# Score rows for the softmax maximum: from the rounded operands alone, in half-array pairs with one reduction for both heads

## The chip, the cores and the metric

The kernel runs on one core of a Trainium2 chip. The metric is the device time of one execution in microseconds. Three runs of the kernel before took 1128.65, 1129.16 and 1133.55 us; the median is 1129.16 us. One further execution was recorded by the profiler: it took 1131.61 us, of which the span from its first to its last instruction is 1129.9 us. Every duration below comes from that one execution.

## The reference

An attention with normalised queries and keys feeds a mixture of experts with one expert per token. Inputs are float32, as is the output.

```
q, k, v: (8, 12, 448, 64)            # batch, heads, sequence, head size
q_n = q / sqrt(mean(q*q) + 1e-6) * g_q ; k_n likewise with g_k
scores = q_n @ k_n.T / 8
scores = scores - max(scores)         # along the keys
attn = exp(scores) ; attn /= sum(attn) + 1e-9
x = (attn @ v), heads side by side    # 3584 tokens of 768
logits = x @ w_gate + modality_bias[modality_id]
e = argmax(logits) ; gate = softmax(logits)[e]
out[token] = gate * (relu(x[token] @ w1[e]) @ w2[e])   # 8 experts, 768 -> 1024 -> 768
```

The maximum that is subtracted cancels when the row is divided by its sum, up to the 1e-9; it only has to be near the true one so that the exponentials stay in range.

## The kernel before

**Attention** runs in 48 units (`NU`), each a pair of heads of one batch element. A unit is worked on over seven steps of a plan, one step for each block `j` of the transposed scores: `st(u, j)` makes 128 rows of keys by 448 queries in PSUM, with the rounded and the remaining parts of the operands and minus the row maximum as an extra row of the contraction (hence matmuls of 65 rows), and ScalarE takes the exponential. Block 3 holds the last 64 keys of each head together. `av(u, c)` multiplies the exponentials with the values in the array's column halves, `sums` and `gates` use its column quarters, `tr` and `xt` transpose, `mt` transposes the maxima.

**The maximum** has to be known before `st` of the same unit, and is made one unit ahead or more by `sa(u, j)` (L810): a second product of queries and keys, not transposed, 128 queries by 448 keys into one PSUM bank, and a VectorE reduction along the keys into column `j` of `mx`. There are seven of them in a unit: three for either head, and one (`j == 3`) that takes the last 64 queries of both heads with a block-diagonal left operand `qm`. For the others the contraction has 128 rows: rows 0 to 63 of `qq` are the rounded queries of head 0, rows 64 to 127 a copy of them that a DMA moved there, and `kk` holds the rounded keys in one half and their remainders in the other. Only unit 0 (`u < PLAN["early"]`) contracts over the 64 rows of the rounded operands alone, because the moved halves would be late there. The left and right operands are `fp32r`, the accumulated scores float32.

**PSUM.** `ps_a` is a pool of two one-bank buffers. Every `sa` takes the next one, and so do `xtr` (the transposes of token rows in the second half, L464), `route_mm` for the last batch element, and the small paths `half_slot` and `small_slot`.

**The order** is written by hand: inside `manual_schedule`, each engine executes in the order in which the Python emits. `put(when("sa", u) + j, "sa", u, jj)` (L1139 to L1142) gives each `sa` its step: unit `u`'s block `j` at step 7u - 14 + j. In a step TensorE gets `st` first, then `sa`, then `av`, `sums`, `gates`, `tr`, `mt`, `xt`; VectorE gets the subtractions and other evacuations that are due, and the reduction of `sa` last. `PLAN` holds the numbers.

**The expert part** follows in 14 slots (`NSTAT`) of 256 tokens, written by hand too, and a tail whose length depends on the data. In a slot `mm1_half` (L485, tile `ph`) makes the hidden layer, `mm2_step` (L515, tile `py`) the output in 16 steps. After steps 9, 11 and 13 `xtr` transposes two of the next slot's six token blocks on TensorE (tile `px`, 128 by 512 in one bank), ScalarE writes the rounded part `xh`, and VectorE the remainder `xl` (tile `xw` in the profile). ScalarE and VectorE split the next slot's weights (`w1w`) in between, in their own program order.

Of the kernel before, what the change touches and what calls it, by code (L numbers as in the profile page):

```python
# [9 lines left out]
F32 = mybir.dt.float32  # L10
# [22 lines left out]
ET = mybir.EngineType  # L33
PLAN = {'rtj': 6, 'rushat': 36, 'av': (1, 1, 4, 6), 'xt': 4, 'xte': (2, 5), 'sm': 2, 'la': 6, 'rc': 9, 'csv': (1,), 'csj': (3, 6), 'csd': (1, 1), 'cse': (2, 1), 'sa': 14, 'mt': 6, 'tk': 21, 'tq': 18, 'nq': 26, 'nk': 26, 'sk': 49, 'sq': 50, 'rs': 48, 'ld': 58, 'first': {('sq', 0): -22, ('sk', 0): -22, ('nk', 0): -21, ('nq', 0): -20, ('sq', 1): -21, ('sk', 1): -21, ('sq', 2): -20, ('sk', 2): -20, ('nk', 1): -18, ('nq', 1): -18, ('tk', 0): -18, ('tq', 0): -18, ('sa', 0): -14, ('tk', 1): -13, ('tq', 1): -11, ('sa', 1): -7, ('mt', 0): -6, ('tk', 2): -8, ('tq', 2): -8, ('nq', 2): -14, ('nk', 2): -14, ('nq', 3): -2, ('nk', 3): -1, ('sq', 3): -8, ('sk', 3): -8, ('sq', 4): -9, ('sk', 4): -9, ('sq', 6): -6, ('sk', 6): -4, ('sk', 7): -7, ('sq', 8): 5, ('sk', 8): 5, ('nk', 7): 15, ('nq', 9): 31, ('tq', 3): 4, ('mt', 1): 0, ('nq', 5): 10, ('mt', 8): 50, ('rs', 0): -21, ('rs', 2): -18, ('nq', 8): 35, ('rs', 5): -7, ('mt', 2): 8, ('nq', 7): 18, ('mt', 5): 30, ('sk', 9): 15, ('tk', 9): 43, ('mt', 6): 36, ('nq', 6): 13, ('sa', 5): 22, ('rs', 7): 0, ('rs', 8): 6, ('mt', 4): 22, ('nk', 4): 4, ('ld', 9): 6, ('tk', 5): 15}, 'rs0': {0: 0, 2: 1, 5: 0, 7: 0, 8: 2}, 'sastep': 1, 'start': -22, 'warm': {5: 2, -6: 16, -12: 4, -7: 2, -9: 4, -21: 4}, 'warmn': 2, 'early': 1, 'late0': 1, 'pmp0': 2, 'ramp': 10, 'pmp': (0, 0, 1, 1, 1, 0, 1), 'nv': [(2, 1)], 'pmpa': (1, 0, 1, 0, 1, 1, 1), 'rush': (1, 1, 1), 'ps': [(7, 1)], 'pa': [(6, 0), (6, 1), (5, 1), (5, 0)], 'rtr': 6, 'sml': 4}
MANUAL = {ET.PE, ET.DVE, ET.Activation, ET.Pool, ET.SP}
# [31 lines left out]
def kernel(  # L67
# [396 lines left out]
    def xtr(s, xr, g):  # L464
        ps = ps_a.tile([128, 2, TB], F32, tag="a", name=f"px{s}_{g}")
        for i in range(2):
            for t in range(2):
                PE.transpose(ps[:, i, 128 * t : 128 * t + 128], xr[t][:, 2 * g + i], idn)  # L468
# [79 lines left out]
    def half_slot(s):  # L548
# [3 lines left out]
        def turn(jj):  # L552
            pt = ps_a.tile([128, 2, TB], F32, tag="a", name=f"pt{s}_{jj}")
# [23 lines left out]
    def small_slot(s, xr):  # L577
# [68 lines left out]
    if True:  # L646
# [162 lines left out]

        def sa(u, j):  # L810
            t = T[u]
            if j == 0:
                t["mx"] = mx_b[u % 2]
            ps = ps_a.tile([128, 512], F32, tag="a", name=f"sa{u}_{j}")
            if j == 3:
                PE.matmul(ps[:, :S], lhsT=qm_b[u % 2], rhs=hi_b[u % 2][1], start=True, stop=True)
            else:
                h = j // 4
                a = 128 * j - h * S
                r = slice(0, 128) if u >= PLAN["early"] else (LO, HI)[h]  # L820
                PE.matmul(ps[:, :S], lhsT=t["qq"][r, h, a : a + 128], rhs=t["kk"][h][r], start=True, stop=True)  # L821
# [301 lines left out]
        def put(n, *what):  # L1123
            plan.setdefault(n, []).append(what)
# [203 lines left out]
        for s in range(NSTAT):  # L1328
# [34 lines left out]
            for b_ in range(16):  # L1363
# [80 lines left out]
```

## Time and profile before

| what | value |
|---|---|
| median of three runs | 1129.16 us |
| the profiled execution, and its span | 1131.61 us, 1129.9 us |
| granted TensorE clock, mean over the span | 0.982 |
| TensorE matmul busy | 1076.3 us, 95% of the span, 6678 instructions |
| TensorE weight load busy | 837.3 us, 74% |
| VectorE busy | 859.6 us, 76%, 1598 instructions |
| ScalarE busy | 824.8 us, 73% |
| GpSimd busy | 662.7 us, 59% |

Attention fills the span up to about 580 us, the expert slots the rest up to about 1098 us, and the tail the last 30 us. A busy share is the union of the recorded durations of an engine. The duration of a matmul includes the time in which its data travel through the array, so that matmuls which follow each other without a gap overlap in the records by more than 0.1 us; what a matmul costs is read from the start of one to the start of the next. The timeline view merges equal neighbours into one row with a count.

### The profile page before, as it was taken

To read this page: it belongs to the slowest core of one execution; us is meant where nothing else is said; L and a number is where in the kernel's file an instruction comes from. 1 tells how busy PE (TensorE), PEld (TensorE's weight loads), DVE (VectorE), ACT (ScalarE), POOL (GpSimd) and SP (SyncE) were. 2 spreads that over 40 slices of the span, in tenths; PEclk is the share of its full clock that TensorE was granted. 3 is DMA by queue.
4 is the path that set the end of the run, shared out by engine and by line. 5 is a ranking of instruction groups with operands and counts; after the bars stand their busy time and mean duration, and the time that the engine had idled before them with its cause. 6 is when DMAs were issued, how large, how long until landed. Compare 5 with 4: busy or idle time off the path is not lost. (4 is left out here: it accounts for less than half of the span.)

```text
span 1129.9 us, 20043 instructions
## 1 busy us (share of the span) xinstructions
PE 1076.3 (95%) x6678; PEld 837.3 (74%) x6678; DVE 859.6 (76%) x1598; ACT 824.8 (73%) x1605; POOL 662.7 (59%) x665
## 2 busy tenths in 40 slices
PE   7799999999999999999999989999999999999993
PEld 6655555555555555555569889999999999999981
DVE  4577788888889877889689978767776677776770
ACT  6778888788778788776677577667876677766870
POOL 4477777778777778787865464354234433445430
PEclk8899999999999999999999999999999999999997
DMA  6656676677667777665823202111160111111360
GB/s 167 156 131 162 144 180 162 167 172 168 154 167 156 168 157 171 152 144 111 238 106 109 43 29 71 29 57 57 43 265 29 58 42 57 32 40 57 109 194 11
DMA packets 127970, 131.79 MB, mean 117 GB/s; under 512 B 68891, under 2 KB 122607, under 8 KB 126320
## 3 DMA queue, kind: packets, MB, share of 16 engines
q1 hardware_dynamic: 110212, 88.58, 33.5%
q0 software_dynamic: 17616, 41.80, 11.7%
q8 instruction: 57, 0.93, 0.4%
q14 instruction: 57, 0.47, 0.1%
q10 hardware_dynamic: 28, 0.01, 0.0%
HBM read 148.74 MB, written 22.38 MB: 151 GB/s over the span
## 5 line engine op out<-in xcount | busy, mean ns | idle before, releaser
L485 PE MATMUL ph<-xw,w1w 128*128 128x256 f32 x2016 | 247.6, 284 | 3.0 <-DVE hlw L52 2.3
L485 PEld LDWEIGHTS ph<-xw,w1w 128*128 128x128 f32 x2016 | 245.4, 193 | 5.0 <-DVE hlw L52 2.5
L52 DVE TENSOR_REDUCE at_hlw<-sa 128x1 f32<-128x448 f32 x336 | 206.7, 617 | 44.5 <-PE sa L821 23.3
L52 DVE TENSOR_TENSOR w1w<-r,w1w 128x256 fp32r<-128x256 f32 x360 | 220.3, 670 | 14.5 <-ACT w1w L52 14.4
L52 ACT CAST w1w<-r 128x256 fp32r<-128x256 f32 x360 | 224.7, 724 | 2.7 <-DMA r<-in_moe_w_dram,ta_wi 2.7
L849 PE MATMUL st<-w1w 128*128 128x448 f32 (+1 forms) x480 | 177.1, 418 | 3.8 <-ACT r2w L52 3.5
L52 ACT ACTIVATE hhw<-ph 128x512 fp32r<-128x512 f32 x56 | 33.5, 597 | 124.8 <-PE ph L485 110.5
L849 PEld LDWEIGHTS st<-w1w 128*128 128x128 f32 (+1 forms) x480 | 85.6, 192 | 48.2 <-ACT r2w L52 21.5
L821 PE MATMUL sa<-w1w 128*128 128x448 f32 (+1 forms) x288 | 110.3, 384 | 9.6 <-DVE at_hlw L52 5.0
L52 ACT ACTIVATE r2w<-st 128x448 f32<-128x448 f32 x168 | 90.1, 542 | 37.6 <-PE st L849 32.1
L52 POOL TENSOR_TENSOR r2w<-r2w 128x448 f32<-128x448 f32 (+1 forms) x72 | 83.4, 1158 | 55.4 <-DVE r2w L52 17.9
L515 PE MATMUL py<-w2lw,hhw 128*128 128x384 f32 x448 | 113.9, 335 | 0.0
L849 PE MATMUL st<-w1w,w2ha 65*128 65x448 f32 x288 | 101.9, 374 | 2.8 <-DMA w1w<-xw 2.5
L52 POOL DMA_INDIRECT out_dram<-yw,lb_oi x22 | 26.8, 1220 | 123.0 <-ACT yw L52 120.0
L52 POOL TENSOR_TENSOR xrw<-r,at_hlw 112x512 f32<-112x512 f32 x95 | 97.4, 1045 | 2.2 <-PE tr L750 1.8
L52 ACT ACTIVATE at_w2lw<-st 128x448 f32<-128x448 f32 x168 | 89.3, 541 | 9.0 <-PE st L849 4.0
L515 PEld LDWEIGHTS py<-w2lw,hhw 128*128 128x128 f32 x448 | 80.9, 188 | 0.0
L52 DVE SCALAR_TENSOR_TENSOR hlw<-ph,hhw 128x512 fp32r<-128x512 f32 x56 | 38.6, 690 | 53.8 <-ACT hhw L52 47.7
L52 ACT ACTIVATE w1w<-tr,gs 64x448 fp32r<-64x448 f32 x96 | 60.4, 629 | 24.8 <-DVE xw L52 24.2
L52 POOL TENSOR_TENSOR r2w<-r2w,at_w2lw 64x448 f32<-64x448 f32 (+1 forms) x48 | 55.4, 1153 | 31.9 <-DVE r2w L52 15.6
L52 ACT ACTIVATE xrw<-r 112x512 f32<-112x512 f32 (+1 forms) x124 | 64.7, 527 | 10.1 <-DMA r<-in_k_dram 7.8
L821 PEld LDWEIGHTS sa<-w1w 128*128 128x128 f32 (+1 forms) x288 | 55.4, 192 | 22.5 <-DVE at_hlw L52 10.2
(297 smaller groups left out, 2300.7 us busy)
## 6 DMA issues: line engine op xcount, KB each, us to landing
w1w<-xw SPq DMA_DIRECT2D x312, 112.0 KB
r<-in_q_dram SPq DMA_DIRECT2D x48, 224.0 KB
r<-in_k_dram SPq DMA_DIRECT2D x48, 224.0 KB
w2ha<-xw SPq DMA_DIRECT2D x72, 112.0 KB
x_d<-at_w2hb SPq DMA_DIRECT2D x8, 672.0 KB
x_d<-yw SPq DMA_DIRECT2D x8, 672.0 KB
r2w<-in_v_dram SPq DMA_DIRECT2D x48, 96.0 KB
at_w2lw<-in_v_dram SPq DMA_DIRECT2D x48, 96.0 KB
```

The costliest lines, as they stand in the source:

```text
L52: return fn(*a, **kw)
L485: PE.matmul(ps[:, i], lhsT=lt_, rhs=rt_[:, c], start=n == 0, stop=n == 17)
L515: PE.matmul(ps[n][:, :384], lhsT=lt_[:, j, 128 * t : 128 * t + 128], rhs=rt_[:, 384 * n : 384 * n + 384], start=j == 0 and m == 0, stop=j ...
L821: PE.matmul(ps[:, :S], lhsT=t["qq"][r, h, a : a + 128], rhs=t["kk"][h][r], start=True, stop=True)
L849: PE.matmul(ps[:, :S], lhsT=l, rhs=t["qq"][:, h] if first else t["ql"][:, h], start=first and (j != 3 or h == 0), stop=not first and (j != ...
```

## The change

Four things change.

1. **`sa` works on both heads at once.** It is called four times a unit instead of seven. For `i` = 0, 1, 2 it issues two matmuls of 64 contraction rows each: head 0 with rows 0 to 63 of `qq` and `kk[0]`, head 1 with rows 64 to 127 of `qq` and `kk[1]`, which are the rounded operands; the remainders of the keys no longer enter the maximum. The two write to the two banks of one tile. Call 3 is the block-diagonal matmul as before.
2. **One reduction for both maxima.** VectorE reduces the two banks in one instruction, 128x2 out of 128x2x448.
3. **The steps.** `sastep` goes, and `'sas': (0, 2, 5, 3)` comes: calls 0, 1, 2 stand in steps 0, 2 and 5 of the seven, the block-diagonal call in step 3. Unit 0 has them in four steps in a row.
4. **One PSUM tile.** The pool `ps_a` has a single buffer `pa` of two banks. `bank_a()` hands out one bank and the other in turn, to call 3 of `sa` and to all other users of the pool.

```diff
-    ps_a = ctx.enter_context(tc.tile_pool(name="ps_a", bufs=2, space=PSUM))
+    ps_a = ctx.enter_context(tc.tile_pool(name="ps_a", bufs=1, space=PSUM))
...
+    pa = ps_a.tile([128, 2, 512], F32, tag="a", name="pa")
+    turn_a = [0]
+    def bank_a():
+        turn_a[0] ^= 1
+        return pa[:, turn_a[0]]
...
     def xtr(s, xr, g):
-        ps = ps_a.tile([128, 2, TB], F32, tag="a", name=f"px{s}_{g}")
+        ps = bank_a().rearrange("p (i t) -> p i t", i=2)
...
-        def sa(u, j):
+        def sa(u, i):
             t = T[u]
-            if j == 0:
+            if "mx" not in t:
                 t["mx"] = mx_b[u % 2]
-            ps = ps_a.tile([128, 512], F32, tag="a", name=f"sa{u}_{j}")
-            if j == 3:
+            if i == 3:
+                ps = bank_a()
                 PE.matmul(ps[:, :S], lhsT=qm_b[u % 2], rhs=hi_b[u % 2][1], start=True, stop=True)
+                o, ps = t["mx"][:, 3:4], ps[:, :S]
             else:
-                h = j // 4
-                a = 128 * j - h * S
-                r = slice(0, 128) if u >= PLAN["early"] else (LO, HI)[h]
-                PE.matmul(ps[:, :S], lhsT=t["qq"][r, h, a : a + 128], rhs=t["kk"][h][r], start=True, stop=True)
+                for h, r in enumerate((LO, HI)):
+                    a = 128 * i + 64 * h
+                    PE.matmul(pa[:, h, :S], lhsT=t["qq"][r, h, a : a + 128], rhs=t["kk"][h][r],
+                              start=True, stop=True)
+                o, ps = t["mx"].rearrange("p (h i) -> p h i", i=4)[:, :, i], pa[:, :, :S]
             def dve():
-                V.tensor_reduce(out=t["mx"][:, j : j + 1], in_=ps[:, :S], op=ALU.max,
-                                axis=AX.X, negate=True)
+                V.tensor_reduce(out=o, in_=ps, op=ALU.max, axis=AX.X, negate=True)
...
-            for j in range(NJ):
-                jj = (0, 1, 2, 4, 5, 6, 3)[j] if u < P["early"] else j
-                put(when("sa", u) + j * (P["sastep"] if u == 0 else 1), "sa", u, jj)
+            for i, j in enumerate(P["sas"] if u >= P["early"] else (0, 1, 2, 3)):
+                put(when("sa", u) + j, "sa", u, i)
```

`half_slot`, `small_slot` and `route_mm` take `bank_a()` in the same way, and `mx` gets an eighth column.

TensorE's order in attention, steps 2, 3 and the start of 4 of a unit that also has `sums` (tile `sm`; `st_2` is block 2 of the scores, `tr` a transpose). Before:

```order
L849 MATMUL st_2_3601<-w1w 128x448
L849 MATMUL st_2_3601<-w1w,w2ha 128x448
L821 MATMUL sa_2_3604<-w1w 128x448
L903 MATMUL sm_3334<-at_w2lw,sel 32x448 x2
L903 MATMUL sm_3334<-at_w2hb,sel 32x448 x2
L849 MATMUL st_3_3618<-w1w 128x448 x2
L849 MATMUL st_3_3618<-w1w,w2ha 128x448 x2
L816 MATMUL sa_3_3623<-xw 128x448
L750 MATMUL tr_0_3625<-idn,xrw 128x112 x4
L849 MATMUL st_4_3633<-w1w 128x448
L849 MATMUL st_4_3633<-w1w,w2ha 128x448
L821 MATMUL sa_4_3636<-w1w 128x448
```

The same place of the change (lines are about ten higher):

```order
L860 MATMUL st_2_3339<-w1w 128x448
L860 MATMUL st_2_3339<-w1w,w2ha 128x448
L831 MATMUL pa<-w1w 128x448 x2
L914 MATMUL sm_3092<-at_w2lw,sel 32x448 x2
L914 MATMUL sm_3092<-at_w2hb,sel 32x448 x2
L860 MATMUL st_3_3356<-w1w 128x448 x2
L860 MATMUL st_3_3356<-w1w,w2ha 128x448 x2
L826 MATMUL pa<-xw 128x448
L758 MATMUL tr_0_3362<-idn,xrw 128x112 x4
L860 MATMUL st_4_3370<-w1w 128x448
L860 MATMUL st_4_3370<-w1w,w2ha 128x448
L899 MATMUL av_3323<-at_w2lw 64x448 x2
```

The pair stands where the single stood in step 2, the block-diagonal matmul still in step 3, and step 4 has lost its `sa`, as steps 1 and 6 have.

VectorE's order over steps 2 to 6 of the same unit, before (`xt` is the evacuation of the transposed result):

```order
L52 TENSOR_REDUCE at_hlw<-sa_2_3604 128x1
L52 TENSOR_REDUCE at_hlw<-sa_3_3623 128x1
L52 TENSOR_TENSOR xw<-tr_0_3625,xw 128x448
L52 TENSOR_REDUCE at_hlw<-sa_4_3636 128x1
L52 TENSOR_TENSOR at_w2hb<-xt_3640,rs_146 112x4x128
L52 TENSOR_REDUCE at_hlw<-sa_5_3659 128x1
L52 TENSOR_REDUCE at_hlw<-sa_6_3672 128x1
```

and in the change:

```order
L52 TENSOR_REDUCE at_hlw<-pa 128x2
L52 TENSOR_REDUCE at_hlw<-pa 128x1
L52 TENSOR_TENSOR xw<-tr_0_3362,xw 128x448
L52 TENSOR_TENSOR at_w2hb<-xt_3375,rs_147 112x4x128
L52 TENSOR_REDUCE at_hlw<-pa 128x2
```

Five reductions became three, two of them over both banks.

TensorE's order in an expert slot around the second of its three `xtr`, with the semaphores that an instruction waits for. Before:

```order
L515 MATMUL py_10_7566<-w2ha,hlw 128x384
L515 MATMUL py_11_7567<-w2ha,hlw 128x384
L468 MATMUL px_1_7622<-idn,xrw 128x128 x4
L515 MATMUL py_10_7566<-w2hb,hhw 128x384
L515 MATMUL py_11_7567<-w2hb,hhw 128x384
L515 MATMUL py_10_7566<-w2lw,hhw 128x384
```

and in the change:

```order
L523 MATMUL py_10_7080<-w2ha,hlw 128x384
L523 MATMUL py_11_7081<-w2ha,hlw 128x384
L476 MATMUL pa<-idn,xrw 128x128 [waits DVE_49]
L476 MATMUL pa<-idn,xrw 128x128 x3
L523 MATMUL py_10_7080<-w2hb,hhw 128x384
L523 MATMUL py_11_7081<-w2hb,hhw 128x384
L523 MATMUL py_10_7080<-w2lw,hhw 128x384
```

Nothing moved, but the second transpose has gained a wait for VectorE. The instruction that it waits for is the VectorE subtraction of the first transpose, which reads the other bank of `pa`; the third likewise waits for the subtraction of the second. Before, only the third waited, for the subtraction of the first, whose buffer it takes.

More of the change, by code (lines that the diff above doesn't have):

```diff
@@ L33 @@
 ET = mybir.EngineType
-PLAN = {'rtj': 6, 'rushat': 36, 'av': (1, 1, 4, 6), 'xt': 4, 'xte': (2, 5), 'sm': 2, 'la': 6, 'rc': 9, 'csv': (1,), 'csj': (3, 6), 'csd': (1, 1), 'cse': (2, 1), 'sa': 14, 'mt': 6, 'tk': 21, 'tq': 18, 'nq': 26, 'nk': 26, 'sk': 49, 'sq': 50, 'rs': 48, 'ld': 58, 'first': {('sq', 0): -22, ('sk', 0): -22, ('nk', 0): -21, ('nq', 0): -20, ('sq', 1): -21, ('sk', 1): -21, ('sq', 2): -20, ('sk', 2): -20, ('nk', 1): -18, ('nq', 1): -18, ('tk', 0): -18, ('tq', 0): -18, ('sa', 0): -14, ('tk', 1): -13, ('tq', 1): -11, ('sa', 1): -7, ('mt', 0): -6, ('tk', 2): -8, ('tq', 2): -8, ('nq', 2): -14, ('nk', 2): -14, ('nq', 3): -2, ('nk', 3): -1, ('sq', 3): -8, ('sk', 3): -8, ('sq', 4): -9, ('sk', 4): -9, ('sq', 6): -6, ('sk', 6): -4, ('sk', 7): -7, ('sq', 8): 5, ('sk', 8): 5, ('nk', 7): 15, ('nq', 9): 31, ('tq', 3): 4, ('mt', 1): 0, ('nq', 5): 10, ('mt', 8): 50, ('rs', 0): -21, ('rs', 2): -18, ('nq', 8): 35, ('rs', 5): -7, ('mt', 2): 8, ('nq', 7): 18, ('mt', 5): 30, ('sk', 9): 15, ('tk', 9): 43, ('mt', 6): 36, ('nq', 6): 13, ('sa', 5): 22, ('rs', 7): 0, ('rs', 8): 6, ('mt', 4): 22, ('nk', 4): 4, ('ld', 9): 6, ('tk', 5): 15}, 'rs0': {0: 0, 2: 1, 5: 0, 7: 0, 8: 2}, 'sastep': 1, 'start': -22, 'warm': {5: 2, -6: 16, -12: 4, -7: 2, -9: 4, -21: 4}, 'warmn': 2, 'early': 1, 'late0': 1, 'pmp0': 2, 'ramp': 10, 'pmp': (0, 0, 1, 1, 1, 0, 1), 'nv': [(2, 1)], 'pmpa': (1, 0, 1, 0, 1, 1, 1), 'rush': (1, 1, 1), 'ps': [(7, 1)], 'pa': [(6, 0), (6, 1), (5, 1), (5, 0)], 'rtr': 6, 'sml': 4}
@@ new lines @@
+PLAN = {'rtj': 6, 'rushat': 36, 'av': (1, 1, 4, 6), 'xt': 4, 'xte': (2, 5), 'sm': 2, 'la': 6, 'rc': 9, 'csv': (1,), 'csj': (3, 6), 'csd': (1, 1), 'cse': (2, 1), 'sa': 14, 'mt': 6, 'tk': 21, 'tq': 18, 'nq': 26, 'nk': 26, 'sk': 49, 'sq': 50, 'rs': 48, 'ld': 58, 'first': {('sq', 0): -22, ('sk', 0): -22, ('nk', 0): -21, ('nq', 0): -20, ('sq', 1): -21, ('sk', 1): -21, ('sq', 2): -20, ('sk', 2): -20, ('nk', 1): -18, ('nq', 1): -18, ('tk', 0): -18, ('tq', 0): -18, ('sa', 0): -14, ('tk', 1): -13, ('tq', 1): -11, ('sa', 1): -7, ('mt', 0): -6, ('tk', 2): -8, ('tq', 2): -8, ('nq', 2): -14, ('nk', 2): -14, ('nq', 3): -2, ('nk', 3): -1, ('sq', 3): -8, ('sk', 3): -8, ('sq', 4): -9, ('sk', 4): -9, ('sq', 6): -6, ('sk', 6): -4, ('sk', 7): -7, ('sq', 8): 5, ('sk', 8): 5, ('nk', 7): 15, ('nq', 9): 31, ('tq', 3): 4, ('mt', 1): 0, ('nq', 5): 10, ('mt', 8): 50, ('rs', 0): -21, ('rs', 2): -18, ('nq', 8): 35, ('rs', 5): -7, ('mt', 2): 8, ('nq', 7): 18, ('mt', 5): 30, ('sk', 9): 15, ('tk', 9): 43, ('mt', 6): 36, ('nq', 6): 13, ('sa', 5): 22, ('rs', 7): 0, ('rs', 8): 6, ('mt', 4): 22, ('nk', 4): 4, ('ld', 9): 6, ('tk', 5): 15}, 'rs0': {0: 0, 2: 1, 5: 0, 7: 0, 8: 2}, 'sas': (0, 2, 5, 3), 'start': -22, 'warm': {5: 2, -6: 16, -12: 4, -7: 2, -9: 4, -21: 4}, 'warmn': 2, 'early': 1, 'late0': 1, 'pmp0': 2, 'ramp': 10, 'pmp': (0, 0, 1, 1, 1, 0, 1), 'nv': [(2, 1)], 'pmpa': (1, 0, 1, 0, 1, 1, 1), 'rush': (1, 1, 1), 'ps': [(7, 1)], 'pa': [(6, 0), (6, 1), (5, 1), (5, 0)], 'rtr': 6, 'sml': 4}
@@ L400 @@
     ra_b, rz_b = SS + 48 * 4, SS + 48 * 5
-    mx_b = [view(sw, SS + 288 + 8 * i, 128, NJ) for i in range(2)]
+    mx_b = [view(sw, SS + 288 + 8 * i, 128, 8) for i in range(2)]
     rs_b = [cp.tile([CP, NCH, 4, 2], F32, name=f"rs{i}") for i in range(2)]
@@ L552, in turn @@
         def turn(jj):
-            pt = ps_a.tile([128, 2, TB], F32, tag="a", name=f"pt{s}_{jj}")
+            pt = bank_a().rearrange("p (i t) -> p i t", i=2)
             for i in range(2):
@@ L584, in small_slot @@
         tk = slice(0, SMALL)
-        px = ps_a.tile([128, 512], F32, tag="a", name=f"qx{s}")
+        px = bank_a()
         for c in range(6):
@@ L609, in small_slot @@
         A.activation(out=hs, in_=ph[:, :TB], func=AF.Relu)
-        pt = ps_a.tile([128, 512], F32, tag="a", name=f"qt{s}")
+        pt = bank_a()
         for i in range(2):
@@ L831, in mt @@
             ps = ps_t.tile([128, 512], F32, tag="t", name=f"mt{u}")
-            PE.transpose(ps[0:NJ, :128], t["mx"], idn)
+            PE.transpose(ps[0:NJ, :128], t["mx"][:, 0:NJ], idn)
             def act():
@@ L996, in route_mm @@
             oh = RT[b]["oh"]
-            ps = pool[0].tile([128, 512], F32, tag=pool[1], name=f"rt{b}")
+            ps = pool[0].tile([128, 512], F32, tag=pool[1], name=f"rt{b}") if pool else bank_a()
             ohf = oh.rearrange("p c e -> p (c e)")
@@ L1370 @@
                 if s == 0 and b_ == 7:
-                    route_mm(B - 1, (ps_a, "a"))()
+                    route_mm(B - 1, None)()
                     small += deferred(lambda: route_pos(B - 1))
```

## The prediction

> **What bounds the kernel now.** I read the windows by stage first, then the groups of one stage, then TensorE's timeline. The windows view gives each engine's busy time in a stretch (with its count of instructions).
>
> ```profile
> core 0: us, PE busy (x) PEld busy (x) DVE busy (x) ACT busy (x) POOL busy (x), PEclk, DMA share, GB/s
> 60.00:560.00 500.00, 488.44 (x2598) 277.93 (x2599) 409.27 (x810) 395.02 (x866) 383.93 (x402) 0.99 0.69 161
> 680.00:1097.00 417.00, 416.65 (x2934) 416.33 (x2933) 309.83 (x472) 302.83 (x462) 174.50 (x147) 1.00 0.24 76
> ```
>
> TensorE is busy for 488 of 500 us in attention and for 416.65 of 417 in the expert slots; VectorE stands at 82% and 74%. So a microsecond of TensorE's order, gained or lost in either stage, is one of the kernel, and a stall there has nothing to hide behind. Next, the TensorE timeline of one unit (start, duration, instruction), to see what a matmul costs from start to start.
>
> ```profile
> 312.80 0.37 PE L849 MATMUL st<-w1w,w2ha 65*128 65x448 f32 x1
> 313.00 0.36 PE L821 MATMUL sa<-w1w 128*128 128x448 f32 x1
> 313.29 0.57 PE L903 MATMUL sm<-at_w2lw,sel 128*32 128x448 f32 x2
> 313.31 0.57 PE L903 MATMUL sm<-at_w2hb,sel 128*32 128x448 f32 x2
> 313.69 0.55 PE L903 MATMUL sm<-at_w2lw,sel 128*32 128x448 f32 x2
> ...
> 314.18 0.68 PE L849 MATMUL st<-w1w 128*128 128x448 f32 x2
> 314.69 0.57 PE L849 MATMUL st<-w1w,w2ha 65*128 65x448 f32 x2
> 315.11 0.37 PE L816 MATMUL sa<-xw 128*128 128x448 f32 x1
> 315.31 0.55 PE L750 MATMUL tr<-idn,xrw 112*128 112x112 f32 x4
> ```
>
> Three readings. Among matmuls that use the whole array a 448-column one costs 0.20 us (312.80 to 313.00, 315.11 to 315.31). Matmuls in different parts of the array run side by side: four `sm` in column quarters start within 0.02 us, and the next four 0.40 us after the first. And the way into another partition of the array costs: `sa` ahead of `sm` takes 0.29 us instead of 0.20, and the first two `st` behind it 0.51 instead of the 0.42 of the next two.
>
> **The pairs.** The change takes three whole-array `sa` out of each unit (six become three pairs) and makes the pairs use row halves. If the two halves overlap as the column parts do, a pair costs one matmul, 0.20 us, and 0.20 us is saved. Against it stands the price of going to row halves and back. The trace has it: unit 0 already contracts over 64 rows, between dummy `warm` matmuls, and a little later the same dummies surround 128-row ones.
>
> ```profile
> 20.64 0.47 PE L821 MATMUL sa<-w1w 64*128 64x448 f32 x1
> 21.05 0.71 PE L1089 MATMUL warm<-idn,ones 128*128 128x128 f32 x4
> 21.69 0.47 PE L821 MATMUL sa<-w1w 64*128 64x448 f32 x1
> ...
> 36.28 0.45 PE L821 MATMUL sa<-w1w 128*128 128x448 f32 x1
> 36.57 0.61 PE L1089 MATMUL warm<-idn,ones 128*128 128x128 f32 x4
> 36.94 0.46 PE L821 MATMUL sa<-w1w 128*128 128x448 f32 x1
> ```
>
> One `sa` and four dummies take 1.05 us with 64 rows and 0.66 with 128: the way in and out costs **0.39 us**. The way out alone, `sa` to dummy, is 0.41 against 0.29, and a dummy waits for nothing. The way in (0.64 against 0.37) could hold a wait of `sa` itself; without it the `sm` rows give a lower bound: 0.09 in, 0.12 out, 0.09 on the first matmul behind, 0.30 in sum. I take 0.39, the row of the very shape. So a pair among whole-array work costs 0.20 + 0.39 = 0.59 us where two singles cost 0.40: **+0.19**. In every second unit the pair of step 2 stands ahead of `sums`, which had to be entered at 0.09 anyway: there 0.09 + 0.40 replaces 0.29 + 0.20, which is 0. Of 3 x 47 = 141 pairs (unit 0 lies among dummies), 118 at 0.19 and 23 at 0 make **+22 us** (12 by the lower bound).
>
> The Trainium skill, page "TensorEngine Tiling (Array Packing)", section Key Properties, says that changing the tiling mode, not just the tile, drains TensorE; it gives no price, and the 0.39 us agrees. Its page "TensorE: Matmul & The Clock Gate", part 3, says that tiles of other rows start about 4 ns apart and speaks of no drain; by it alone the 141 pairs would save 0.20 us each, 28 us, which is the second rival below. That pure row halves overlap no row of this trace shows. The bounds are 0.20 us a pair (side by side, as `sm`) and 0.40 (one after the other); I take 0.20.
>
> **The reductions.** VectorE trades six reductions for three of twice the length.
>
> ```profile
> L52 DVE TENSOR_REDUCE at_hlw<-sa 128x1 f32<-128x448 f32 x310 | 190.8, 617 | 39.5 <-PE sa L821 20.5 <-PE sa L816 15.6 <-issue 1.9
> L52 DVE TENSOR_REDUCE at_hlw<-xrw 112x8 f32<-112x512 f32 x78 | 52.6, 675 | 0.4 <-ACT xrw L52 0.3
> ```
>
> 64 more elements cost 58 ns, so 448 more cost about 0.41 us by that slope; twice the row would be 1.23. Both ends stand: 1.02 to 1.23 us, and I take 1.05, nearer the slope. That is 6 x 0.617 - 3 x 1.05 = 0.55 us a unit, 26 us of VectorE in all, which is not the bound and so is worth only what TensorE waited for it:
>
> ```profile
>   DVE at_hlw L52: 13.2, 16
> ```
>
> This is the row of line L821 in 60 to 560 us: 16 waits of `sa` for a reduction, 13.2 us. With a lighter VectorE and longer units I take half of it away, **-6 us**, bounds 0 and -13.
>
> The two-bank tile brings a wait too. The block-diagonal matmul of step 3 must wait for the reduction of the pair of step 2. Without `sums` between them, it comes up 0.40 (pair) + 0.51 + 0.42 (four `st`) = 1.33 us after the pair's start; the reduction ends at 0.47 + 1.05 and some 0.08 us of hand-over, 1.60. So it waits some 0.28 us in 24 units, **+7 us** (0 to 17), with `tr` and the next `st` queued behind it. With `sums` (0.89 us) between them there is no wait. Attention in sum: 22 - 6 + 7 = **+23 us**.
>
> **The expert slots.** No instruction is added here, but the second transpose of a slot now waits for VectorE's subtraction of the first, and `py` stands behind it. Timelines of TensorE, VectorE and ScalarE in one slot:
>
> ```profile
> 843.67 0.68 PE L468 MATMUL px<-idn,xrw 128*128 128x128 f32 x4
> 846.30 0.68 PE L468 MATMUL px<-idn,xrw 128*128 128x128 f32 x4
> ...
> 844.48 0.68 DVE L52 TENSOR_TENSOR xw<-px,xw 128x512 fp32r<-128x512 f32 x1
> 847.31 0.72 DVE L52 TENSOR_TENSOR xw<-px,xw 128x512 fp32r<-128x512 f32 x1
> ...
> 845.97 0.61 ACT L52 CAST xw<-px 128x512 fp32r<-128x512 f32 x1
> ```
>
> The second transpose went at 843.67; the first one's subtraction ended at 845.16. It would now start at 845.21, 1.54 us late. ScalarE takes the second at 845.97 anyway, so its subtraction still ends at 848.03, while the third transpose, 2.63 us behind the second, would come at 847.84 and so goes at 848.08: **1.78 us** later than before. Nothing hides it, and the next slot has the same order and, by the chain of waits (start, duration, what), the same period, 35.53 us:
>
> ```profile
> 706.95 17.27 PE ph L485 x144
> ...
> 742.48 17.27 PE ph L485 x144
> ```
>
> So it comes again in each of the 11 slots from 680 to 1062 us: **+19.6 us**. The two slots ahead of them have more waiting, and partly slack:
>
> ```profile
> 621.94 0.80 PE L468 MATMUL px<-idn,xrw 128*128 128x128 f32 x4 [0.33 <-DVE rtc L52]
> 626.34 0.81 PE L468 MATMUL px<-idn,xrw 128*128 128x128 f32 x4 [1.48 <-DVE xw L52]
> 631.40 15.98 PE L485 MATMUL ph<-xw,w1w 128*128 128x256 f32 x131 [0.62 <-DVE xw L52]
> 664.19 0.81 PE L468 MATMUL px<-idn,xrw 128*128 128x128 f32 x4 [1.16 <-DVE xw L52]
> 678.31 10.39 PE L485 MATMUL ph<-xw,w1w 128*128 128x256 f32 x72 [2.28 <-DVE hlw L52]
> ...
> 628.93 0.70 DVE L52 TENSOR_TENSOR xw<-px,xw 128x512 fp32r<-128x512 f32 x1
> ```
>
> In the first, the second transpose moves from 621.94 to 626.3 and the third from 626.34 to 629.7 (the subtraction of the second ends at 629.63): 3.4 us, less the 0.62 us that `ph` waited, 2.8. In the next, a similar 2.8 mostly falls into the 2.28 us that `ph` waits at 678.31: 0.5. With about 1 us in the last slot (bounds 0 and 2.8) the expert part costs 19.6 + 2.8 + 0.5 + 1 = **+24 us**.
>
> **Sum.** 23 + 24 = +47 us, from the profiled execution's 1131.61 us to 1178.6. That execution lies 2.45 us above the median of 1129.16, so I forecast **1176 us**.
>
> **Rivals.**
> - *The halves do not overlap.* Each pair then costs 0.20 us more, 28 us in 141: **1204 us**. For it: no row shows row halves together. Against it: column parts overlap within 0.02 us.
> - *The switch is hidden between row halves and `st`.* Then a pair saves 0.20 us, and attention comes to -28 - 6 + 7 = -27 instead of +23: **1126 us**, the expert waits eating nearly all of it. Against it stands the 0.39 us above.
> - *The expert wait costs nothing*, because VectorE comes to its subtraction earlier than before. Then only attention counts: **1152 us**. Against it: VectorE's order in the slots is unchanged, and its pace there is set by the weights that ScalarE splits ahead of it.
> - *Faster:* both of the last two, a hidden switch and hidden waits: -27 us, **1102 us**. It turns faster by over 0.5% where the switch costs under 0.15 us and the slots lose under 0.5 us each.
> - *The change does not do what it says*: the pairs might be placed in the same rows. Then they follow each other, as in the first rival; their operands start at partitions 0 and 64, which speaks against it.
>
> **How the numbers follow.** The forecast 66% (1152 to 1194 by its terms' bounds), no overlap 11%, hidden switch 9%, hidden expert wait 8%, both 4%, others 2%. The range 1146 to 1206 takes in the forecast, no overlap and the hidden expert wait, 85%. A difference of 0.5% (5.6 us) is about what a measurement of this kernel tells from none. Faster by more: 4% and a quarter of the hidden switch, 7%; within: most of the rest of that, 6%; slower: 87%.
>
> **What would show it.** In attention, the two matmuls of a pair within 0.02 us of each other, a first `st` some 0.4 us behind them, and the `st` ahead of a pair at 0.29 us: overlap and the price of the switch. A unit without routing work longer by about 0.5 us. In a slot, the second `px` (now `pa`) marked as released by VectorE's `xw`, some 1.5 us late, and a slot period of 37.3 instead of 35.5 us (by the starts of `ph`). I am wrong if `st` follows a pair after 0.21 us, if the two starts lie 0.2 us apart, or if the slots keep their period.

## The result, and the profile after

The changed kernel takes **1176.97 us** (median of 4 runs, 1175.51 to 1177.87), the kernel before took 1130.51 us on the same chip (1128.65 to 1133.55, 4 runs). The ratio is 1.0378, with a 95% interval of 1.0346 to 1.0409: 46 us slower, where 1176 us was forecast. The profiled executions are 1177.87 us (span 1176.2) after and 1131.61 us (span 1129.9) before.

The same windows as before, for the stage that they then covered (columns as in the prediction):

```profile
60.00:560.00 500.00, 485.89 (x2493) 232.86 (x2492) 393.06 (x664) 382.02 (x840) 367.36 (x388) 0.99 0.65 150
```

In 500 us TensorE starts 105 matmuls fewer than before (2493 against 2598, 4% less) and is as busy (486 us against 488): the same time carries less work. VectorE's 393 us against 409 are the same 4% and show no relief by themselves. Over the whole execution its busy time fell from 859.6 to 852.9 us (the pages), 7 us; the prediction's 26 add up single durations, which overlap in the records.

To see where the time went I take the starts of `mt`, one in each unit. First the four units between the ninth and the thirteenth `mt`, which in every kernel of this study but one (e11 below) have no stalls except those that come in all units of their kind, then the first and the last `mt` of all. TensorE's timeline, before:

```profile
34.95 0.28 PE L832 MATMUL mt<-idn,at_hlw 128*7 128x128 f32 x1 [0.94 <-ACT w1w L52]
...
124.22 0.28 PE L832 MATMUL mt<-idn,at_hlw 128*7 128x128 f32 x1
...
167.54 0.28 PE L832 MATMUL mt<-idn,at_hlw 128*7 128x128 f32 x1
...
564.88 0.28 PE L832 MATMUL mt<-idn,at_hlw 128*7 128x128 f32 x1
```

and after:

```profile
34.96 0.28 PE L843 MATMUL mt<-idn,at_hlw 128*7 128x128 f32 x1 [1.13 <-ACT w1w L52]
...
124.20 0.28 PE L843 MATMUL mt<-idn,at_hlw 128*7 128x128 f32 x1
...
169.95 0.28 PE L843 MATMUL mt<-idn,at_hlw 128*7 128x128 f32 x1
...
585.76 0.28 PE L843 MATMUL mt<-idn,at_hlw 128*7 128x128 f32 x1
```

The four units took 43.32 us and take 45.75. All 47 intervals took 529.9 us and take 550.8, **20.9 us** more. What lies above 47 quarters of the four units is called the excess below (the start, irregular stalls and stretches of a lower clock); it fell from 20.9 to 13.2 us. Inside a unit, steps 2 and 3 where there is no `sums`, first on TensorE and then on VectorE:

```profile
334.05 0.37 PE L860 MATMUL st<-w1w,w2ha 65*128 65x448 f32 x1
334.34 0.47 PE L831 MATMUL pa<-w1w 64*128 64x448 f32 x2
334.74 0.68 PE L860 MATMUL st<-w1w 128*128 128x448 f32 x2
335.25 0.57 PE L860 MATMUL st<-w1w,w2ha 65*128 65x448 f32 x2
336.00 0.47 PE L826 MATMUL pa<-xw,w2ha 128*128 128x448 f32 x1 [0.18 <-DVE at_hlw L52]
336.31 0.55 PE L758 MATMUL tr<-idn,xrw 112*128 112x112 f32 x4
```

```profile
334.86 1.09 DVE L52 TENSOR_REDUCE at_hlw<-pa 128x2 f32<-128x896 f32 x1 [1.09 <-PE pa L831]
336.51 0.62 DVE L52 TENSOR_REDUCE at_hlw<-pa 128x1 f32<-128x448 f32 x1 [0.56 <-PE pa L826]
```

The pair (two matmuls in one row of 0.47 us, 3 to 4 ns apart in the records) is entered after 0.29 us and left after 0.40, then the two `st` behind it take 0.51. The block-diagonal matmul could start at 335.25 + 0.42 = 335.67. It starts at 336.00, after the pair's reduction has ended at 335.95, and lets `tr` follow after 0.31 us, not the 0.20 that a whole-array matmul costs when nothing stalls.

In the expert slots, TensorE's transposes of one slot, with the `py` row behind each:

```profile
721.19 0.68 PE L476 MATMUL pa<-idn,xrw 128*128 128x128 f32 x4
721.63 0.59 PE L523 MATMUL py<-w2ha,hhw 128*128 128x384 f32 x2
...
725.52 0.81 PE L476 MATMUL pa<-idn,xrw 128*128 128x128 f32 x4 [1.56 <-DVE xw L52]
726.08 0.60 PE L523 MATMUL py<-w2hb,hhw 128*128 128x384 f32 x2
...
728.34 0.81 PE L476 MATMUL pa<-idn,xrw 128*128 128x128 f32 x4
728.90 0.60 PE L523 MATMUL py<-w2hb,hhw 128*128 128x384 f32 x2
```

The second transpose waits for VectorE, as forecast. In the chain of waits the slots now come 37.54 us apart, where they came 35.53 apart:

```profile
731.23 17.27 PE ph L493 x144
...
768.77 17.27 PE ph L493 x144
```

The span grew by 46.3 us: 20.9 in attention; 0.4 between the last `mt` and the first `ph`; 2.94 in the first slot; 0.08 in the next two together; ten times 2.00; and 2.02 from the start of the last slot to the end.

### The profile page after: what moved, and what is told of

Read it like the earlier page. It is cut to its first block, busy times and chain, and to the rows that moved or that the text cites. A ratio compares the mean times of both kernels' runs of the same rounds, so it can differ in the third digit from the quotient of the medians.

```text
span 1176.2 us, 19912 instructions
## 1 busy us (share of the span) xinstructions
PE 1099.8 (94%) x6678; PEld 797.6 (68%) x6678; DVE 852.9 (73%) x1454; ACT 826.4 (70%) x1605; POOL 668.2 (57%) x665
## 4 chain that ended last, share of the span: by engine, by line
PE 68%; DVE 12%; ACT 9%; DMA 5%; issue 3%; SPq 1%; POOL 1%; ACTq 0%; DVEq 0%; POOLq 0%
PE ph L493 17%; PE av L899 13%; PE st L860 12%; PE py L523 9%; ACT w1w L52 6%; PE pa L831 4%; DVE at_hlw L52 4%; PE tr L758 3%; DMA lt<-l_d,tb_li 3%; DVE w1w L52 3%; PE xt L956 2%; PE pa L476 2%; PE sm L914 2%; PE pa L826 1%; DVE xw L52 1%
## 5 line engine op out<-in xcount | busy, mean ns | idle before, releaser
L52 DVE TENSOR_REDUCE at_hlw<-pa 128x2 f32<-128x896 f32 x192 | 186.5, 971 | 68.9 <-PE pa L831 43.5
L860 PE MATMUL st<-w1w 128*128 128x448 f32 (+1 forms) x480 | 183.3, 432 | 2.7 <-ACT r2w L52 1.5
L860 PEld LDWEIGHTS st<-w1w 128*128 128x128 f32 (+1 forms) x480 | 82.0, 190 | 59.0 <-ACT r2w L52 21.0
L52 ACT ACTIVATE at_w2lw<-st 128x448 f32<-128x448 f32 x168 | 89.9, 542 | 17.7 <-PE st L860 15.8
L52 POOL DMA_INDIRECT out_dram<-yw,lb_oi x22 | 24.0, 1093 | 126.9 <-ACT yw L52 123.9
L52 DVE TENSOR_TENSOR w2lw<-r2w,w2ha 128x1536 fp32r<-128x1536 f32 x28 | 49.1, 1758 | 44.8 <-ACT w2ha L52 44.8
L831 PE MATMUL pa<-w1w 64*128 64x448 f32 x288 | 68.7, 469 | 4.3 <-DVE at_hlw L52 3.5
L52 DVE TENSOR_REDUCE at_hlw<-xrw 112x8 f32<-112x512 f32 x91 | 61.2, 678 | 14.9 <-ACT xrw L52 14.9
```

The lines of the kernel that those rows point to most:

```text
L52: return fn(*a, **kw)
L831: PE.matmul(pa[:, h, :S], lhsT=t["qq"][r, h, a : a + 128], rhs=t["kk"][h][r], start=True, stop=True)
L860: PE.matmul(ps[:, :S], lhsT=l, rhs=t["qq"][:, h] if first else t["ql"][:, h], start=first and (j != 3 or h == 0), stop=not first and (j != ...
```

## The experiments

All of them are variants of the changed kernel, and each was timed against the kernel before on its own chip (medians of before 1129.27 to 1130.96 us). "Four units" and "attention" are read from the starts of `mt`, "slot" from those of `ph`, in the profiled execution. The excess is attention less 47 quarters of the four units; two executions with the same attention part (after and e1, e5 and e6) differ in it by 2 to 3 us. The profiled executions of e2 and e5 lie 6.5 and 3.7 us below their medians, that of e11 4.4 above, and the four units of e11 hold one irregular wait of 0.41 us.

| run | time, us | ratio (95%) | four units | attention | excess | slot |
|---|---|---|---|---|---|---|
| before | | 1 | 43.32 | 529.9 | 20.9 | 35.53 |
| after | 1176.97 | 1.0378 (1.0346 to 1.0409) | 45.75 | 550.8 | 13.2 | 37.53 |
| e1 own tiles in the slots | 1148.04 | 1.016 (1.0115 to 1.0204) | 45.75 | 548.0 | 10.4 | 35.53 |
| e2 whole rows | 1173.28 | 1.0389 (1.0341 to 1.0437) | 44.55 | 540.9 | 17.5 | 37.5 |
| e3 steps 1, 4, 6, 2 | 1181.92 | 1.0478 (1.0421 to 1.0534) | 46.45 | 555.3 | 9.6 | 37.5 |
| e4 two reductions a pair | 1174.51 | 1.0406 (1.0357 to 1.0455) | 45.87 | 545.8 | 6.8 | 37.5 |
| e5 steps 0, 2, 4, 6 | 1167.3 | 1.0322 (1.0267 to 1.0377) | 44.14 | 536.7 | 18.1 | 37.5 |
| e6 = e5 and own tiles | 1140.72 | 1.0084 (1.0054 to 1.0115) | 44.14 | 538.9 | 20.2 | 35.53 |
| e7 = e6 with whole rows | 1150.51 | 1.0154 (1.0071 to 1.0237) | 43.33 | 546.7 | 37.6 | 35.53 |
| e8 both in one half | 1200.52 | 1.0616 (1.0562 to 1.067) | 48.20 | 569.8 | 3.4 | 37.5 |
| e9 own tiles, steps 1, 4, 6, 3 | 1134.74 | 1.0041 (1.0023 to 1.0059) | 43.42 | 533.3 | 23.1 | 35.53 |
| e10 = e7 with steps 2, 4, 6, 0 | 1137.38 | 1.0075 (1.0048 to 1.0102) | 43.44 | 536.7 | 26.3 | 35.53 |
| e11 = e9, block-diagonal call apart | 1135.97 | 1.0049 (1.0025 to 1.0074) | 43.92 | 538.7 | 22.6 | 35.53 |
| e12 = e11, in step 5 | 1141.25 | 1.0105 (1.0062 to 1.0148) | 44.47 | 540.2 | 17.7 | 35.53 |

**e1: two one-bank tiles again, but for the expert part alone.** The pool of the two-bank tile is closed with the last unit, and its banks go to a pool of two.

```diff
 def bank_a():
+    if ps_x:
+        turn_a[0] += 1
+        return ps_x[0].tile([128, 512], F32, tag="x", name=f"pb{turn_a[0]}")
     turn_a[0] ^= 1
     return pa[:, turn_a[0]]
+def own_tiles():
+    own_a.close()
+    ps_x.append(ctx.enter_context(tc.tile_pool(name="ps_x", bufs=2, space=PSUM)))
...
+    if n == NJ * (NU - 1):
+        own_tiles()
```

> The change, but the two-bank tile is given up at the end of attention, and the transposes of the expert slots and the other later users get two one-bank buffers again. If the wait of each slot's transposes on the other bank's subtraction is what the slots lose, the slot period returns from 37.53 us to 35.5 and the time falls by 25 us, from 1177 to about 1152; attention (first to last transpose of the maxima, 550.8 us in the change, 529.9 before) stays at 551. The rival, that the slots are slower because the longer attention leaves ScalarE or VectorE in another phase, keeps the period at 37.5 and the time at 1177.

1148.04 us. TensorE's transposes of a slot come evenly again (2.61 and 2.63 us apart), and the slots every 35.53 us:

```profile
716.59 0.68 PE L484 MATMUL pb<-idn,xrw 128*128 128x128 f32 x4
...
719.20 0.68 PE L484 MATMUL pb<-idn,xrw 128*128 128x128 f32 x4
...
721.83 0.68 PE L484 MATMUL pb<-idn,xrw 128*128 128x128 f32 x4
```

The bank that a transpose writes is not the one that VectorE's subtraction still has to read; only the dependency on the whole tile made it wait. From the first `ph` to the end the kernel before takes 548.4 us, the changed kernel 573.3 and e1 545.4: the expert part's 25 us are back, and 3 more, 2.2 of them in the second and third slot.

**e2: whole rows in the pairs.** Each matmul of a pair contracts over 128 rows, so that no half of the array is entered or left; tile, reduction and steps stay.

```diff
 for h, r in enumerate((LO, HI)):
     a = 128 * i + 64 * h
+    if u >= PLAN["early"]:
+        r = slice(0, 128)
```

> The change, but both matmuls of a pair use all 128 rows (rounded queries twice, rounded keys and their remainders), as before; pairing, steps, the single reduction and the tile stay. If the way into row halves and back costs 0.39 us and overlap gives 0.20 back, 118 pairs give up 0.19 us each, 22 us: attention 529, the time 1155, the slots unchanged at 37.53. The rival, that attention lost its 21 us to the longer reductions and to waits for the shared tile, leaves attention at 545 to 551 and the time at 1172 to 1177.

Half a miss: in the profiled execution attention came to 540.9 us, so 10 of the 22 us returned. That execution is the fastest of four; by the medians under 4 us returned, and the ratio cannot be told from that of the changed kernel. The four units, which don't hang on this, fell by 1.20 us, 14 in 47 units. TensorE's timeline at the same place shows what kept the rest:

```profile
326.63 0.58 PE L833 MATMUL pa<-w1w 128*128 128x448 f32 x2
327.05 0.57 PE L862 MATMUL st<-w1w 128*128 128x448 f32 x2
327.46 0.58 PE L862 MATMUL st<-w1w,w2ha 65*128 65x448 f32 x2
328.39 0.47 PE L826 MATMUL pa<-xw,w2ha 128*128 128x448 f32 x1 [0.36 <-DVE at_hlw L52]
```

Pair and `st` no longer lose anything (0.42, 0.41), but the second matmul of the pair ends 0.20 us later and its reduction with it, so the block-diagonal matmul, which could go at 327.88, goes at 328.39. Its waits grew from 8.5 to 14.8 us (60 to 560 us). In units with `sums` between the two, the time is that of the kernel before (11.04 and 11.42 us from `mt` to `mt`, against 11.05 and 11.42); in the others it is 0.62 us longer. Switch and wait are in part interchangeable, which I had not reckoned with: with the switch gone, the next wait is late.

**e3: each pair directly ahead of `av`**, which has to enter column halves anyway: `'sas': (1, 4, 6, 2)`.

> The change with its calls in steps 1, 4 and 6, each just ahead of the value product, which uses column halves and needs a switch anyway, and the block-diagonal call in step 2. If the price is one of switches and not of pairs, every pair shares its way out with the product behind it: 118 times 0.19 us and the 7 us wait of the block-diagonal call go, attention about 523 to 529, the time about 1149 to 1155. The rival, that each pair costs its 0.59 us wherever it stands, saves only the wait: attention 544, the time 1170.

A miss: slower than the changed kernel. The switches are shared as meant (first two rows below: `av` 0.40 us behind the pair), but the block-diagonal matmul, in step 2 now, comes late. TensorE, then VectorE:

```profile
326.38 0.47 PE L831 MATMUL pa<-w1w 64*128 64x448 f32 x2
326.78 1.72 PE L899 MATMUL av<-at_w2lw 128*64 128x448 f32 x8
...
329.95 0.47 PE L826 MATMUL pa<-xw 128*128 128x448 f32 x1 [0.84 <-DVE at_hlw L52]
```

```profile
327.62 0.68 DVE L52 SCALAR_TENSOR_TENSOR xw<-tr,gs,xw 128x448 fp32r<-128x448 f32 x1 [0.99 <-ACT xw L52]
328.22 0.68 DVE L52 TENSOR_REDUCE at_hlw<-xrw 112x8 f32<-112x512 f32 x1
328.81 1.08 DVE L52 TENSOR_REDUCE at_hlw<-pa 128x2 f32<-128x896 f32 x1
```

The pair of step 1 is done by 326.85, but its reduction stands third in VectorE's queue, behind a subtraction that waits 0.99 us for ScalarE. This wait came 38 times, 25.7 us in 60 to 560 us.

**e4: two reductions of one bank for each pair**, as many and as long as before the change.

```diff
-V.tensor_reduce(out=o, in_=ps, op=ALU.max, axis=AX.X, negate=True)
+for h in range(2):
+    V.tensor_reduce(out=o[:, h : h + 1], in_=ps[:, h], op=ALU.max, axis=AX.X, negate=True)
```

> The change with two reductions of one bank each behind every pair in place of the one over both. VectorE gets some 20 to 26 us of work back. If VectorE is not the bound, only the wait of the block-diagonal call grows, by 0.1 to 0.2 us in 24 units, 3 to 5 us, and a few waits in units with routing: 1177 to 1184. The rival, that VectorE's relief carries weight in attention, gives 1190 or more.

1174.51 us, no different (the intervals overlap). The single instruction for both maxima brings nothing that this measurement can tell.

**e5: even steps**, `'sas': (0, 2, 4, 6)`, which puts the block-diagonal call two steps behind a pair and one pair ahead of `av`.

> The changed kernel with the calls of sa in steps 0, 2, 4 and 6 instead of 0, 2, 5 and 3: the block-diagonal call now lies two steps behind the pair before it, and the third pair stands directly ahead of av, which has to switch to column halves anyway. Theory (the 21 us that attention lost are the switch to row halves and back, plus the wait of the block-diagonal matmul for the pair's reduction): the waits of line L826 fall from 8.5 us to under 2 us, and one switch in three is shared with av (47 x 0.19 = 9 us), so attention (first to last mt) falls from 551 to about 533 us and the time from 1177 to about 1159 us. Rival (attention lost its time to something else, such as VectorE's longer reductions): 1172 us or more. The slots keep their 37.5 us.

In the profiled execution attention fell by 14 of the expected 18 us, the median of the time by 9.7. In the four units 1.61 us went, 18.9 us over 47 units as worked out; the excess grew by 4.9 us. The waits of the block-diagonal matmul fell to 2.5 us.

**e6: even steps and own tiles.**

> Steps 0, 2, 4 and 6, row halves, and in the expert part two one-bank tiles as in the kernel before. If the two causes are independent, their gains add: 18 us in attention and 29 us in the slots, 1177 - 18 - 29 = about 1130 us, the kernel before within 0.5%, with a slot period of 35.5 us. Rival (what is gained in attention is lost again before the first slot, or the other way round): 1140 us or more.

1140.72 us, by which the rival's figure holds: the sum of the expected gains is short by 10 us. The rival's reason does not: from the last `mt` to the first `ph` e6 takes 16.7 us, the changed kernel 17.1. Against e5 the slots, their tail and the passage to them gave 26.5 us, while attention took 2.1 us more with the same four units. By the medians e1 had gained 28.9 us and e5 9.7 (not 18), 38.6 together, and e6 gained 36.3. So the causes add, and the shortfall is that of e5; the excess is what moves.

**e7: as e6, with whole rows.**

> As the run before it, but the pairs contract over all 128 rows as the kernel before did: no switch, and one reduction for both maxima. Theory: the pair of step 0 and, in every second unit, that of step 2 lose 0.19 us each (47 + 23 pairs, 13 us), the others nothing, since sums and av have to be entered anyway: about 1117 us, which is also the kernel before without its 13 us of waits of sa for reductions. Attention from first to last mt: about 520 us. Rival (the price of the switch goes into other waits, as it half did with whole rows in steps 0, 2, 5, 3): 1130 us, no gain over the run before it.

The largest miss, 33 us. The four units take 43.33 us, as in the kernel before, but the excess is 37.6 us. (The expectation also takes the prediction's 13 us of waits for what TensorE could win; the part on the prediction shows that it is 4.3.) The waits (TensorE, 35 to 580 us: total, times, longest), and the worst place in the timeline:

```profile
PE pa L841 <- DMA w1w<-xw: 7.4, 6, 3.3
```

```profile
372.87 0.44 PE L841 MATMUL pa<-w1w 128*128 128x448 f32 x1
376.61 0.71 PE L841 MATMUL pa<-w1w 128*128 128x448 f32 x1 [3.31 <-DMA w1w<-xw]
```

The second matmul of a pair waits for the DMA that moves the remainders of head 1's keys into the other half of `kk`. Before the change, head 1 came four steps later. A contraction over the 64 rows of the rounded operands needs no moved half: that is a side of the change which the prediction does not have, and which e7 had given up.

**e8: both matmuls in rows 0 to 63.** The second takes head 0's operands again, so head 1's maxima are not computed.

```diff
-PE.matmul(pa[:, h, :S], lhsT=t["qq"][r, h, a : a + 128], rhs=t["kk"][h][r],
+if u >= PLAN["early"]:
+    r, h0, a = LO, 0, 128 * i
+PE.matmul(pa[:, h, :S], lhsT=t["qq"][r, h0, a : a + 128], rhs=t["kk"][h0][r],
```

> The changed kernel with both matmuls of a pair in rows 0 to 63: the second takes the operands of head 0 again, so the maxima of head 1 are replaced by those of head 0 and the output is not the reference's. The switch, the tile, the reduction and the steps stay. Theory (the two halves run side by side, at the price of one matmul): the second now starts 0.20 us behind the first, 141 x 0.20 = 28 us more, about 1205 us, less where the wait of the block-diagonal matmul hides it. Rival (the 4 ns between their starts are only in the records, and the two take the array one after the other): 1177 us, no change.

A pair now costs 0.60 us to the next `st`, where it costs 0.40 in row halves:

```profile
345.15 0.67 PE L835 MATMUL pa<-w1w 64*128 64x448 f32 x2
345.75 0.67 PE L864 MATMUL st<-w1w 128*128 128x448 f32 x2
```

The four units grew by 2.45 us, 0.20 for each of their twelve pairs, and the time by 24 us: less than 28, as the excess fell to 3.4 us. So in the changed kernel the halves do run side by side, and that is worth 0.20 us a pair, as taken.

**e9: own tiles, steps 1, 4, 6, 3**: e3 with the block-diagonal call one step later.

> Two one-bank tiles in the expert part, row halves, and the calls of sa in steps 1, 4, 6 and 3: all three pairs stand directly ahead of av and share its switch, and the block-diagonal matmul of step 3 comes two steps behind the pair of step 1, not one as in the run with steps 1, 4, 6, 2. Theory (what attention lost is unshared switches and the wait of the block-diagonal matmul for the pair's reduction): four undisturbed units, which took 45.79 us in the changed kernel and 44.13 with steps 0, 2, 4, 6, take about the 43.32 us of the kernel before; attention from first to last mt about 530 us, slots 35.5 us, 1130 us in all, the kernel before within 0.5%. Rival (the pair of step 1 still has its reduction behind work that VectorE can't begin, as in steps 1, 4, 6, 2): four units 46 us or more, and 1145 us or more.

1134.74 us, ratio 1.0041. The four units take 43.42 us, 0.10 more than before the change:

```profile
124.14 0.28 PE L851 MATMUL mt<-idn,at_hlw 128*7 128x128 f32 x1
...
167.57 0.28 PE L851 MATMUL mt<-idn,at_hlw 128*7 128x128 f32 x1
```

With three steps changed in the plan and two tiles in the slots, the half-array pairs cost nearly what the six whole-array matmuls cost. All but some 4 of the 46 us are thus the places of the four calls (the switches and the wait of the block-diagonal matmul together) and the tile in the slots.

**e10: as e7, with the pairs in steps 2, 4, 6 and the block-diagonal call in step 0**, so that the moved halves are needed two steps later.

> The run with whole rows in steps 0, 2, 4, 6 gave 1150 us where 1117 was expected. Its four undisturbed units took 43.33 us, exactly those of the kernel before, but its pairs waited 7.4 us for DMAs that move the remainders of the keys into the other half of kk, 3.31 us at once where one came late, which contractions over the 64 rows of the rounded operands don't need. Here the same kernel has its pairs in steps 2, 4, 6 and the block-diagonal call in step 0, so that the moved halves are needed two steps later. Theory (whole rows wait for the moves because head 1's operands are now needed with head 0's): waits of the pairs for DMA under 2 us, attention from first to last mt about 530 us instead of 547, and about 1130 us. Rival (the lost time has nothing to do with the moves): 1145 us or more, with attention at 542 us or more.

The pairs no longer wait for the moves at all (the view has one wait of a pair for a DMA, 0.9 us, and that for a load of `v`), and attention fell by 10 of the expected 17 us. But `st` now waits 3.2 us in four places for DMAs of the same name, which neither theory has. The time, 1137.38 us, lies between the two theories' figures. It fits with the moves being most of e7's loss, but the places of the calls changed as well, so that their share alone is not shown.

**e11 and e12: the block-diagonal call takes a buffer of the transposes' pool**, in step 3 (e11) or 5 (e12).

```diff
-ps = bank_a()
+ps = ps_t.tile([128, 512], F32, tag="t", name=f"sa{u}_{i}")
```

> As the run with own tiles and steps 1, 4, 6, 3, but the block-diagonal matmul writes to a buffer of the pool that the transposes use, so that neither it nor the pair behind it waits for the other's reduction. In that run the pairs waited 8.7 us in 18 places for VectorE and the block-diagonal matmul 3.5 us. Theory (these waits come from the tile of two banks that both share): nearly all 3.5 us and about half of the 8.7 us go, and four undisturbed units take 43.2 us instead of 43.45; about 1127 us. Rival (the transposes now wait for the reduction of the block-diagonal matmul, or the stalls return elsewhere): 1133 us or more.

> As the run before it, with the block-diagonal call in step 5 instead of 3: the one step in which the transposes' pool has no other user, between the pairs of steps 4 and 6. Theory: as the run before it, about 1127 us, and no wait of a transpose for its reduction. Rival (its reduction stands in VectorE's queue ahead of the next pair's, which comes later for it): 1133 us or more.

Neither came to 1127 us. In e11 the pairs' waits for VectorE fell from 8.7 to 3.5 us, as meant, but the transposes took up waits for VectorE's reductions, which e9 does not have:

```profile
PE tr L766 <- DVE at_hlw L52: 3.8, 3, 1.8
PE pa L839 <- DVE at_hlw L52: 3.5, 5, 1.0
...
PE xt L964 <- DVE at_hlw L52: 2.1, 1, 2.1
```

In e12 it is the block-diagonal matmul that waits, 3.8 us in four places, for ScalarE's work on the transposes' buffers. No version beat the kernel before; e9 comes nearest.

## Why the prediction was right

**The price of the switch** was taken as 0.39 us in and out, 0.19 more a pair than two whole-array matmuls. e6 against e7, which differ in the rows alone, gives it by itself: 44.14 against 43.33 us, 0.81 in four units. The pair of step 4, ahead of `av`, is taken to cost nothing; in the two units with `sums` only the pair of step 0 is then left, 0.10 us; in the two without, 0.30, so 0.20 for the pair of step 2. After against e2 gives another 0.20 for the pair of step 5 (0.30 in units with `sums`). In sum 47 x (0.10 + 0.20) + 24 x 0.20 = **19 us** where 22 was forecast; the pair ahead of `tr` was overpriced by half. The Trainium skill, "TensorEngine Tiling (Array Packing)", section Key Properties, says that a change of the tiling mode drains TensorE, and gives no price; e6 and e7 agree with it.

**The wait of the block-diagonal matmul** was taken as 0.28 us in 24 units, 7 us. In e2, where nothing is switched, it is 0.62 us; with row halves the pair ends 0.20 us earlier, which leaves 0.42, **10 us**. The rows above show 0.33 of wait, and 0.31 instead of 0.20 us for the matmul that had stalled: this second part was missing. The reduction took 1.088 us (mean), not 1.05.

**Fewer waits, -6 us**: the excess fell by 7.7. The size is near, but that is luck, as the row behind the term was misread. Its 13.2 us and 16 waits add up the matmuls of line L821 and their weight loads (PEld). Four waits are counted twice, once for either; in the other eight places, of weight loads alone, no matmul waits for a reduction. The waits of 60 to 560 us (total, times, longest), before:

```profile
PEld sa L821 <- DVE at_hlw L52: 8.9, 12, 1.9
PE sa L821 <- DVE at_hlw L52: 4.3, 4, 1.5
PE sa L821 <- DMA w1w<-xw: 3.4, 5, 1.0
```

and after:

```profile
PE pa L826 <- DVE at_hlw L52: 8.5, 23, 2.9
PE pa L831 <- DVE at_hlw L52: 2.0, 3, 0.8
```

So there were 4.3 us to win and 2.3 were won. Of the waits for the moved halves, 3.4 us, none is left; but e2, which needs the moved halves, has only 0.2 us of them, so that the rows alone do not explain this either. 4.5 of the 7.7 us lie in the first four units, which took 46.8 us before and take 44.7. Nor is the lighter VectorE the reason: e4 gives VectorE its old reductions back, and its excess is lower still.

What the table shows is that the excess falls as the four units get longer, from 21 to 26 us at 43.3 to 43.4 down to 3 us at 48.2 (e7 apart). From e8 to e10 the 47 units' regular time falls by 56 us and attention by 33; from e8 to the kernel before by 57 and 40. So 0.6 to 0.7 of a microsecond saved in TensorE's order arrives, and not the whole one of which the prediction's first section speaks. What keeps back the rest was not tried, and stays open.

Attention in sum: 19 + 10 - 8 = 21 us, forecast 23.

**The expert slots** were forecast at 1.78 us each and measured at 2.00. Before, the third transpose came 5.24 us behind the first (841.06 in the slot whose next two the prediction quotes, 846.30), now it comes 7.15 behind (721.19, 728.34): 1.91 us late, 0.13 more than forecast, because VectorE's second subtraction, on which it waits, ends that much later. And it takes 0.56 us to the next `py`, where the first one, which waited for nothing, takes 0.44. That is 2.03. Against it, the two slots behind the first lost 0.08 us together and not 0.5 + 1.78. The earlier of them took 2.38 us more, and the 2.28 us wait at 678.31 covered that, as forecast. What the forecast left out is the clock: behind that wait the granted clock was 0.84 on average (678.3 to 688.7 us), and 72 matmuls took the 10.39 us that the prediction's row shows, where 72 in a slot after take 8.64. With the wait this stretch went too, so that the later slot, with its own stall, takes 37.57 us, before 39.87. First slot 2.94 (2.8), last slot and tail 2.02 (1). In sum 25 us, forecast 24. e1 shows that the mechanism is the tile.

**The rivals.** *No overlap* is what e8 looks like, and it is not the change. *A switch that is hidden* is refuted by the rows and by e6 against e7. *An expert wait at no cost* is refuted by the slot period, and with it *Faster*. The change does what it says.

The mechanisms were right: overlap, switch, wait of the block-diagonal matmul, wait in the slots. That the sum came within 1 us of the measured time is partly luck, as several terms missed by 2 to 3 us, in both directions: 22 for 19 and 7 for 10 in attention, 2.2 us too little in ten slots and 2.2 too much in the two ahead of them.

## What to carry to other kernels

Two half-array matmuls side by side cost as much as one, but among whole-array work the way in and out cost more than that gain; put them next to other work that leaves the whole array anyway. When two buffers are made one tile, every user of either waits for the readers of both, also in stages that the change does not mean to touch. Before taking a cost away, look for what is late next: here a freed switch became a wait, and a freed wait a stall elsewhere.

## What the runs showed of the hardware that was not expected

- With the way in and back, a pair in row halves costs 0.20 us more than the same two matmuls over all rows ahead of `st`, 0.10 more ahead of `tr`, and nothing ahead of `av` or `sums`, which have to be entered from the whole array in any case (e6 against e7, after against e2).
- In one unit of e7 TensorE waited 1.19 and then 3.31 us, and ran at half the clock from 374.1 to 380.9 us. The unit took 18.12 us, where others of its kind take 11.05: 7.1 us more for 4.5 us of waits (windows view; the columns as in the prediction, the granted clock is the third number from the end):

```profile
363.30:374.00 10.70, 8.82 (x47) 4.84 (x45) 6.31 (x9) 7.57 (x20) 10.07 (x14) 1.00 0.54 139
374.10:380.90 6.80, 4.29 (x13) 2.29 (x15) 2.46 (x4) 2.49 (x5) 4.14 (x5) 0.50 0.62 122
```

  The Trainium skill, "TensorE: Matmul & The Clock Gate", part 1, has the rate halved after an idle window of some 3.4 us. Here the clock fell 0.8 us into the longer wait, which began at 373.30, so that this wait by itself was not that window; what the clock went by this trace does not show.
- One reduction out of two banks took 1.088 us (the group's mean, after), two out of one bank 0.617 each (before): 0.146 us less for a pair.

```profile
L52 DVE TENSOR_REDUCE at_hlw<-pa 128x2 f32<-128x896 f32 x144 | 156.7, 1088 | 47.8 <-PE pa L831 43.5
```
